# Batch 1 in units of 256 tokens, expert 1 from half-block 8 of batch 1 on, and constant matmuls where TensorE waits in batches 0 and 1

## The chip, the cores and the metric

The kernel runs on one core of one Trainium2 chip. The engines of the core are TensorE (PE, matmuls), VectorE (DVE), ScalarE (ACT), GpSimd (POOL) and SyncE (SP, which here only issues transfers). Each engine works through its own list of instructions in the order of the program and waits on semaphores for the others. The metric is the device time of one execution in microseconds (us).

## What is computed

Eight batches of sliding-window attention with ALiBi, whose output rows are the tokens of a mixture of eight experts; the expert weights come from a Sinkhorn normalisation over all tokens.

```python
batch, n_heads, seq, head_dim = (8, 8, 576, 64)
scores = scale * np.matmul(q, k.transpose(0, 1, 3, 2))
mask = (rel >= 0) & (rel < window)                      # window = 128
scores = np.where(mask, scores + bias[None], -1000000000.0)
attn = np.exp(scores - max); attn = attn / sum
x = matmul(attn, v), as (4608, 512)

P = np.exp(logits)                                      # logits = x @ w_gate, (4608, 8)
for _ in range(8):
    P /= P.sum(1, keepdims=True) + 1e-09
    P /= P.sum(0, keepdims=True) + 1e-09
    P *= N / E
for e in range(E):                                      # w1[e] (512, 1024), w2[e] (1024, 512)
    h = np.maximum(x @ w1[e], 0.0)
    out += P[:, e:e + 1] * (h @ w2[e])
```

Inputs and output are fp32; the matmuls of the kernel take fp16 and accumulate in fp32.

## The kernel before

**Attention.** A batch has 576 tokens, that is four blocks of 128 and one of 64 (kb 0 to 4). Each block is worked in two half-blocks (u) of four heads, so a batch has ten half-blocks; `at = 2 * kb + u` counts them from 0 to 9, and the text writes (b, at). A half-block goes through `scores` (L363, TensorE: keys by queries into the PSUM tile psS), `exps` (L386, ScalarE: exp into pt), `masks` (L398, VectorE: pt times a table that holds both the ALiBi factor and the window), `values` (L409, TensorE: pt by V into psN, where a column of ones gives the sum; VectorE divides into xsb) and, after both halves of a block, `turn_x` (L447), which transposes the block into xT, the input of the experts. For batches 0, 1, 2 and 7 this transpose is done by TensorE (psX, copied by VectorE); for the others by a transposing DMA.

**Getting q, k and v ready.** `load_qk` (L228) loads a batch's q and k in fp32 on the SP queue; `cast_qk` (L237) casts a quarter j of both to fp16, q on VectorE and k on ScalarE; `turn_pe` (L302) transposes one quarter of one of them on TensorE into psT, and ScalarE copies k, VectorE copies q to its place (kN, qN). Batches 0, 1 and 2 go this way; later ones are transposed by DMA. `turn_pe` with j = 4 (NDT) turns the batch's tail of 64 tokens, which ScalarE copies to tT. `load_v` (L330, SP) and `cast_v` (L340, POOL) bring V.

**Experts as filler.** Experts 0 and 1 are worked during attention, in units of some blocks of one expert. A unit (`unit_atoms`, L91) is eight layer-1 steps (`l1`, L97: four matmuls into psh, evicted by ScalarE with a Relu to hT) and one layer-2 step per block (`l2`, L111: eight matmuls into psy, evicted by VectorE in `keep`, L491). `spans` (L502) are the units' blocks, and `order` alternates expert 0 with expert 1 two units behind. `Filler` (L147) hands the steps out: a unit may start when its blocks are ready (`filler.ready`) and its expert is allowed (`filler.allowed`); `fill(us)` issues steps until their planned costs (0.87 us for layer 1 of four blocks, less in proportion for fewer; 1.74 us for layer 2) make up the asked time.

**The order around the change.** The loop over half-blocks (`steps`) issues, in this order: scores of what comes next, its exp, 1 us of filler, its mask, the values of this half-block, the transposes of the block before, the V cast, and then the rest of a budget. The budget is the backlog of filler divided by the half-blocks left up to (b, 8); so at the end of (b, 8) all filler that is ready has been used. Behind the budget stand the events of a half-block: `filler.ready` is raised at every block (L659 to L664), expert 1 is allowed and the first four results are stored at (1, 4), batch 2 is loaded at (0, 3), cast from (1, 3) to (1, 6) and turned from (1, 4) to (1, 7), and the casts of batch b + 2 come at (b, 8), (b, 9) and the two half-blocks after, for b from 1 on.

**Buffers.** The pool `pmm` has four PSUM banks, given out in turn to psT, psN, psX, psh, psy and others; psS has two larger ones. The fp32 loads of V and of the tails share five buffers (`s32`); the large q and k buffers share eight (`a8`).

**After attention** come the Sinkhorn rounds, with the rest of the filler between them, and then experts 2 to 7 in 108 units of 256 tokens (L801 and on).

Of the kernel before, what the change touches and what calls it, by code (L numbers as in the profile page):

```python
# [9 lines left out]
FP16 = mybir.dt.float16  # L10
FP32 = mybir.dt.float32
# [3 lines left out]
def kernel(  # L15
# [10 lines left out]
    nc = tc.nc  # L26
# [9 lines left out]
    P = 128  # L36
# [3 lines left out]
    GT = 512  # L40
    NG = Ntok // GT
# [27 lines left out]
    ident = per.tile([P, P], FP16, name="ident")  # L69
    ident32 = per.tile([P, P], FP32, name="ident32")  # L70
    ones32 = per.tile([P, P], FP32, name="ones32")
    wg_sb = per.tile([P, NDT, E], FP16, name="wg_sb")
    rs_sb = per.tile([P, NBLK], FP32, name="rs_sb")
    cs_sb = per.tile([P, E], FP32, name="cs_sb")
# [72 lines left out]
    class Filler:  # L147


        def __init__(self, units):  # L150
            self.todo = list(units)
            self.l1: list = []
            self.l2: list = []
            self.l1_us = 0.0
            self.since = 0
            self.ready = 0
            self.allowed = {0}

        def start_unit(self):
            for n, (e, b0, nb, make) in enumerate(self.todo):  # L160
# [7 lines left out]
        def take(self):  # L168
            if not self.l1 and len(self.l2) <= 2:
                if self.start_unit():  # L170
                    self.since = 0
            use_l2 = bool(self.l2) and (not self.l1 or self.since >= 2)
            if use_l2:
                self.l2.pop(0)()
                self.since = 0
                cost = L2_US
            elif self.l1:
                self.l1.pop(0)()
                self.since += 1
                cost = self.l1_us  # L180
                if not self.l1:
                    self.l2 = self.l2 + self.next_l2
            else:
                return 0.0
            return cost
# [14 lines left out]
    aps = ctx.enter_context(tc.tile_pool(name="aps", bufs=1, space=bass.MemoryType.PSUM))  # L200
    first_pool = ExitStack()
    asb = first_pool.enter_context(tc.tile_pool(name="asb", bufs=1))
    if True:
# [12 lines left out]
        KT: dict = {}  # L216
        QKT: dict = {}
        vs: dict = {}

        def load_tail(b):  # L220
            t32 = asb.tile([P, H, Dh], FP32, name=f"t32_{b}", tag="s32", bufs=5)
# [187 lines left out]
        def values(b, kb, u):  # L409

            nk, _ = sizes(kb)
            if u == 0:
                xsbs[b, kb] = asb.tile([P, H, Dh], FP16, name=f"xsb_{b}_{kb}", tag="xsb", bufs=3)
            psN = aps.tile([P, GT], FP32, name=f"psN_{b}_{kb}_{u}", tag="pmm", bufs=4)
            psN = psN[:, 0 : 4 * Dh + 4].rearrange("p (h d) -> p h d", h=4)
            ops = []
            for y in range(2):
                for hb in range(2):
                    hh = 2 * y + hb
                    if kb > 0:  # L420
                        ops.append((hh, pts[b, kb - 1, u][:, 2 * hb + y, P : P + nk], vs[b, kb - 1][:, 4 * u + hh, 0 : Dh + 1]))
                    ops.append((hh, pts[b, kb, u][0:nk, 2 * hb + y, 0:nk], vs[b, kb][0:nk, 4 * u + hh, 0 : Dh + 1]))
            if kb == NKB - 1:
                ops = ops[0::2] + ops[1::2]
            for i, (hh, lhsT, rhs) in enumerate(ops):
                nc.tensor.matmul(  # L426
                    out=psN[0:nk, hh, :],
                    lhsT=lhsT,
                    rhs=rhs,
                    start=(i == 0),  # L430
                    stop=(i == len(ops) - 1),
                )
            if kb > 0:
                pts.pop((b, kb - 1, u))
            rden = asb.tile([P, 4], FP32, name=f"rden_{b}_{kb}_{u}", tag="rden", bufs=2)
            nc.vector.reciprocal(out=rden[0:nk, :], in_=psN[0:nk, :, Dh])
            nc.vector.tensor_tensor(
                out=xsbs[b, kb][0:nk, 4 * u : 4 * u + 4, :],
                in0=psN[0:nk, :, 0:Dh],
                in1=rden[0:nk, :].unsqueeze(2).to_broadcast([nk, 4, Dh]),  # L440
                op=ALU.mult,
            )
# [56 lines left out]
            nc.vector.tensor_copy(out=yo, in_=ps)  # L499
            stores.append((e, blk, yo))  # L500

        spans = [(0, 2), (2, 2)] + [(4 * g, 4) for g in range(1, NG)]  # L502
        order = [(0, 0), (0, 1)]
        for n in range(2, len(spans)):
            order += [(0, n), (1, n - 2)]
# [87 lines left out]
        nc.scalar.dma_start(out=rel, in_=rel_h.ap())  # L593
        nc.scalar.dma_start(out=ident, in_=ident_h.ap())
        nc.scalar.dma_start(out=ident32, in_=ident32_h.ap())
        load_first()
        nc.vector.memset(ones32, 1.0)
        make_mask(0)
        cast_v(0)
        load_weights(0, 0, 1)  # L600
# [11 lines left out]
        steps = [(b, kb, u) for b in range(B) for kb in range(NKB) for u in range(2)]  # L612
        for j in range(2):
            cast_qk(0, j)
            turn_pe(0, 1, j)
            turn_pe(0, 0, j)
        cast_qk(0, 2)
        cast_qk(0, 3)
        scores(*steps[0])
        exps(*steps[0])  # L620
        turn_pe(0, 1, 2)
        turn_pe(0, 0, 2)
        masks(*steps[0])
        turn_pe(0, 1, 3)
        turn_pe(0, 0, 3)
        make_mask(1)
        for n, (b, kb, u) in enumerate(steps):
            nxt = steps[n + 1] if n + 1 < len(steps) else None
            at = 2 * kb + u
            left = ((8 if b < XPE else 10) - at) % 10 + 1  # L630
            budget = filler.backlog() / (11 if (b, at) == (XPE, 0) else left)
            if nxt:
                if nxt[0] < XPE and nxt[1:] == (RI - 2, 1):
                    turn_pe(nxt[0], 0, NDT)
                if nxt == (1, 0, 0):
                    cast_qk(1, 0)
                    cast_qk(1, 1)
                    for j in range(NDT):
                        turn_pe(1, 1, j)
                        turn_pe(1, 0, j)  # L640
                        if j < 2:
                            cast_qk(1, j + 2)
                        filler.fill(1.0)
                if n == 0:
                    scores(*nxt)
                elif nxt[2] == 0:
                    scores(*nxt)
                    scores(*nxt[:2], 1)
                exps(*nxt)
            got = filler.fill(1.0)  # L650
            if nxt:
                masks(*nxt)
            values(b, kb, u)
            if n > 0 and u == 0 and by_pe(steps[n - 1][0]):
                turn_x(*steps[n - 1][:2])
            if u == 1 and n // 2 + NKB < B * NKB:
                cast_v(n // 2 + NKB)
            filler.fill(budget - got)
            if at == 0 and b > XPE:  # L659
                filler.ready = 4 * b  # L660
            if at < 8 and b < XPE:
                filler.ready = 4 * b + at // 2
            if at == 8 and b < XPE:
                filler.ready = 4 * b + 4  # L664
            if u == 1 and not by_pe(b):
                turn_x(b, kb)
            if u == 1:
                if kb == 1 and b > 0:
                    gates(4 * b - 4, 4 * b)
                if n // 2 + NKB + 1 < B * NKB:  # L670
                    load_v(n // 2 + NKB + 1)
            if b == 0 and at == 1:
                load_weights(1)
            if b == 1 and at == 4:
                filler.allowed.add(1)
                nc.sync.dma_start(out=ysp[0, 0:RI].rearrange("m p d -> p m d"), in_=first_y[0])
            if (b, at) == (0, 3):
                load_qk(2)
            if (b, at) == (0, 7):
                homes(1)  # L680
            if (b, at) == (1, 3):
                homes(2)
            if b == 1 and 3 <= at <= 6:
                cast_qk(2, at - 3)
            if b == 1 and 4 <= at <= 7:
                turn_pe(2, 1, at - 4)
                turn_pe(2, 0, at - 4)
            if 1 <= b < B - 2 and at == 3:
                load_qk(b + 2)
            if 1 <= b < B - 2 and at >= 8:  # L690
                cast_qk(b + 2, at - 8)
            if 2 <= b < B - 1:
                if at < 2:
                    cast_qk(b + 1, at + 2)
                if at == 1:
                    turn_qk(b + 1)
                    order_qk(b + 1, 1, range(NDT))
                if at == 5:
                    turn_tail(b + 1)
                if at in (6, 7):  # L700
                    order_qk(b + 1, 0, range(2 * at - 12, 2 * at - 10))
            if b < B - 1 and at == (1 if b > 1 else 5) and b:
                load_tail(b + 1)
            if 10 * b + at >= 66:
                i = 10 * b + at - 66
                if i % 8 == 0:
                    home_last(2 + i // 8)
                (load_w2 if i % 8 < 4 else load_w1)(2 + i // 8, i % 4, 4)
            if (b, at) == (7, 0):
                todo += sums_of(2, *extras(2))  # L710
            if b == 7 and at >= 5:
                some(1)
# [30 lines left out]
        for it in range(8):  # L743
# [4 lines left out]
                out=P_sb,  # L748
# [298 lines left out]
```

## Time and profile before

| | |
|---|---|
| median of three runs | 1058.99 us (1057.99 to 1059.68) |
| the profiled execution, its time | 1060.31 us |
| its span, first to last instruction | 1058.5 us |
| PE busy | 1031.1 us (97%), 9006 matmuls |
| DVE, ACT, POOL busy | 631.7, 434.5, 77.4 us |
| DMA | 98.55 MB, mean 93 GB/s |
| ACT evictions of layer 1, 128x512 and 128x256 (36 to 160 us) | mean 599 and 386 ns |

Busy time of PE is the time in which at least one matmul is under way; matmuls are pipelined, so the duration of a group of n matmuls is n times their distance plus the time that the last one takes to drain. The clock in the profile is the share of TensorE's full clock that the throttle granted. A row of the timeline gives start and duration in us, engine, line, operation, output and inputs, shapes and how many instructions were merged; in brackets stands how long the engine was idle before it and what ended that.

### The profile page before, as it was taken

The page shows a single profiled execution, that of the slowest core. Times are in us where ns is not written, and L with a number is a line of the kernel's source. Part 1 is how long each engine was busy: PE and PEld are TensorE (multiplying, and loading weights), DVE is VectorE, ACT ScalarE, POOL GpSimd, SP SyncE. Part 2 cuts the span into 40 slices and gives each one's busy share as a digit, 9 for nine tenths or more (in the row PEclk, how much of TensorE's full clock was granted, in tenths as well). Part 3 has the DMA queues.
Part 4 walks back from the last instruction along what each step waited for, and adds up shares of the span by engine and source line. Part 5 has one row for each costly group of instructions (what it writes and reads, how often), then busy time and mean ns, then how long its engine had stood idle before and what let it go on. Part 6 is the DMA issues. An engine that isn't in the chain of part 4 may idle for free.

```text
span 1058.5 us, 21148 instructions
## 1 busy us (share of the span) xinstructions
PE 1031.1 (97%) x9006; PEld 802.9 (76%) x9006; DVE 631.7 (60%) x1171; ACT 434.5 (41%) x729; POOL 77.4 (7%) x139
## 2 busy tenths in 40 slices
PE   6789999999999999999999999999999999999998
PEld 4455444444544888888888888888888888888887
DVE  4655665655687665655655655655655655555555
ACT  6556555555233333333333333333333333333332
POOL 2112032325100000000000000000000000000000
PEclk9999999999999999999999999999999999999999
DMA  9985599879992501211211210211220220220240
GB/s 226 252 221 139 114 201 218 196 154 177 182 207 70 115 23 49 71 26 46 71 39 33 70 49 23 71 39 32 71 65 7 71 68 3 71 71 1 71 90 20
DMA packets 166110, 98.55 MB, mean 93 GB/s; under 512 B 84960, under 2 KB 157440, under 8 KB 166016
## 3 DMA queue, kind: packets, MB, share of 16 engines
q1 hardware_dynamic: 151280, 79.21, 29.4%
q0 software_dynamic: 14304, 17.84, 10.2%
q8 instruction: 70, 1.15, 0.4%
q14 instruction: 24, 0.20, 0.1%
q10 hardware_dynamic: 432, 0.16, 0.1%
HBM read 87.74 MB, written 19.02 MB: 101 GB/s over the span
## 4 chain that ended last, share of the span: by engine, by line
PE 92%; DMA 4%; SPq 2%; DVE 1%; ACT 1%; issue 0%; POOL 0%; ACTq 0%
PE psh L834 36%; PE psS_m L889 31%; PE psh L102 11%; PE psy L115 10%; DMA v<-in_v_dram 2%; DMA k<-in_k_dram 2%; PE psN L426 1%; PE psS L372 1%; DMA xT<-xsb 1%; SPq L334 1%; SPq L223 0%; SPq L288 0%; PE psy L954 0%; PE psG L473 0%; ACT hT L109 0%
## 5 line engine op out<-in xcount | busy, mean ns | idle before, releaser
L841 ACT ACTIVATE hs<-psh 128x512 f16<-128x512 f32 x432 | 258.0, 597 | 453.2 <-PE psh L834 373.7
L834 PE MATMUL psh<-aux,w1l 128*128 128x256 f16 x2880 | 372.6, 273 | 0.2 <-ACT hs L841 0.2
L834 PEld LDWEIGHTS <-w1l 128*128 128x128 f16 x2880 | 281.7, 98 | 33.3 <-issue 0.5
L889 PEld LDWEIGHTS <-hs 128*128 128x128 f16 x2568 | 251.3, 98 | 29.1
L846 DVE TENSOR_TENSOR hs<-hs 128x1024 f16<-128x1024 f16 x107 | 74.1, 693 | 274.5 <-ACT hs L841 274.3
L889 PE MATMUL psS_m<-w2l,hs 128*128 128x256 f16 x1440 | 186.6, 273 | 0.0
L102 PE MATMUL psh<-xT,w1t 128*128 128x512 f16 (+1 forms) x640 | 141.1, 359 | 4.4 <-DMA xT<-xsb 1.7
L115 PE MATMUL psy<-w2t,hT 128*128 128x512 f16 x576 | 133.8, 379 | 3.4 <-DMA w2t<-in_moe_w_dram 2.8
L818 DVE TENSOR_TENSOR aux<-xT,pbc 128x1024 f16<-128x1024 f16 x108 | 131.4, 1217 | 2.5 <-DMA pbc<-ptd 2.5
L109 ACT ACTIVATE hT<-psh 128x512 f16<-128x512 f32 (+1 forms) x160 | 87.6, 556 | 100.6 <-PE psh L102 99.3
L115 PEld LDWEIGHTS <-hT 128*128 128x128 f16 x576 | 53.7, 98 | 64.6 <-issue 4.8
L102 PEld LDWEIGHTS <-w1t 128*128 128x128 f16 x640 | 57.9, 99 | 53.6 <-issue 6.4
L390 ACT ACTIVATE pt<-psS 128x1024 f16<-128x1024 f32 (+2 forms) x80 | 67.5, 852 | 45.9 <-PE psS L372 37.0
L935 DVE TENSOR_TENSOR acc<-acc,psS_m 128x256 f32<-128x256 f32 (+1 forms) x162 | 74.3, 504 | 12.4 <-PE psS_m L889 11.1
L499 DVE CAST yo<-psy 128x512 f16<-128x512 f32 x68 | 46.9, 690 | 55.5 <-PE psy L115 54.3
L403 DVE TENSOR_TENSOR pt<-pt,mask 128x1024 f16<-128x1024 f16 (+2 forms) x80 | 50.2, 627 | 41.5 <-ACT pt L390 41.4
L889 PE MATMUL psS_m<-more,hs 128*128 128x256 f16 x576 | 74.6, 273 | 0.0
L834 PE MATMUL psh<-aux,w1t 128*128 128x256 f16 x576 | 74.6, 273 | 0.0
L849 DVE TENSOR_TENSOR hs<-hs 128x1024 f16<-128x1024 f16 x107 | 73.2, 684 | 0.0
L834 PEld LDWEIGHTS <-w1t 128*128 128x128 f16 x576 | 56.4, 98 | 6.5
L535 POOL DMA_DIRECT2D w2t<-in_moe_w_dram x2 | 1.8, 878 | 705.2 <-PE psS_m L889 669.8
L426 PEld LDWEIGHTS <-pt 128*128 128x128 f16 (+2 forms) x576 | 28.6, 101 | 26.1 <-DVE pt L403 6.8
(83 smaller groups left out, 657.2 us busy)
## 6 DMA issues: line engine op xcount, KB each, us to landing
pbc<-ptd SPq DMA_DIRECT2D x108, 128.0 KB, 4.5
y<-ysp SPq DMA_DIRECT2D x36, 256.0 KB, 4.7
ysp<-yo SPq DMA_DIRECT2D x68, 128.0 KB, 3.1
v<-in_v_dram SPq DMA_DIRECT2D x32, 256.0 KB, 3.9
out_dram<-acc SPq DMA_DIRECT2D x31, 256.0 KB, 2.4
q<-in_q_dram SPq DMA_DIRECT2D x7, 1024.0 KB, 6.4
k<-in_k_dram SPq DMA_DIRECT2D x7, 1024.0 KB, 9.8
w2t<-in_moe_w_dram POOLq DMA_DIRECT2D x4, 1024.0 KB, 14.7
```

What stands on the lines that cost most here:

```text
L102: nc.tensor.matmul(out=ps[:, 0:nt], lhsT=w1ts[e][:, dt, P * ft : P * ft + P], rhs=xT[:, b0 : b0 + nb, dt, :], start=(dt == 0), stop=(dt == ...
L109: nc.scalar.activation(out=st["hT"][:, ft, 0:nt], in_=ps[:, 0:nt], func=AF.Relu)
L115: nc.tensor.matmul(out=ps, lhsT=st["hT"][:, ft, P * ms : P * ms + P], rhs=w2ts[e][:, ft, :], start=(ft == 0), stop=(ft == NFT - 1),)
L390: nc.scalar.activation(out=pt[0:nk, :, 0 : nk + nn], in_=ps[0:nk, :, :, 0 : nk + nn].rearrange("p a y n -> p (a y) n"), func=AF.Exp, scale ...
L403: nc.vector.tensor_tensor(out=pt[0:nk, :, 0:w], in0=pt[0:nk, :, 0:w], in1=mask[0:nk, hs, 0:w], op=ALU.mult)
L818: nc.vector.tensor_tensor(out=xs(n).rearrange("p (d b t) -> p d b t", d=NDT, b=2), in0=xT[:, 2 * g : 2 * g + 2].rearrange("p b d t -> p d ...
L834: nc.tensor.matmul(out=ps[:, f, :], lhsT=W1L[e][:, dt, P * ft : P * ft + P], rhs=xs(n)[:, HB * dt : HB * dt + HB], start=(dt == 0), stop=( ...
L841: nc.scalar.activation(out=h[n][:, 2 * i : 2 * i + 2, :], in_=ps, func=AF.Relu)
L846: nc.vector.tensor_tensor(out=t[:, NFT : NFT + NF2, :], in0=a[:, 0:NF2, :], in1=a[:, NF2:NFT, :], op=ALU.add)
L849: nc.vector.tensor_tensor(out=t[:, NFT + NF2 : 2 * NFT, :].rearrange("p f n -> p (f n)").rearrange("p (f t) -> p f t", t=P), in0=a[:, :, P ...
L889: nc.tensor.matmul(out=Ms[g, bank][:, half, :], lhsT=left(n, m, f), rhs=W2L[e][RIGHT[m]][:, f, :], start=(e == 2 and f == 0 and half == 0) ...
L935: nc.vector.tensor_tensor(out=a, in0=a, in1=p2, op=op)
```

## The change

- A tile `junk` is made: ones32 read as fp16, 128 x 256. `spin(ps, n)` issues n matmuls of junk by junk, 256 wide, into a given PSUM tile; `spin_alone(n)` does so into a bank of its own from the pool `pmm`. Nobody reads the results. The memset of ones32 moves ahead of the first loads.
- Constant matmuls are issued: 20 at the start, four at each of four places among the first turns, score and masks of batch 0, six ahead of the first layer-2 step, three ahead of each of the four turns of batch 1, and four in `values`, into psN ahead of its own matmuls, in every half-block of batch 0 and in half-blocks 0 to 5 of batch 1. That is 118 in all.
- The four blocks of batch 1 are two units of two blocks instead of one of four, for both experts.
- Expert 1 is allowed at the end of (1, 8) instead of (1, 4).
- The casts of batch 2 move from (1, 3) to (1, 6), one quarter each, to (1, 5) (two quarters), (1, 6) and (1, 7); its turns move from (1, 4) to (1, 7) to (1, 6) (two quarters), (1, 7) and (1, 8), and stand ahead of the casts in each half-block.

```diff
@@ the tiles
     ones32 = per.tile([P, P], FP32, name="ones32")
+    junk = ones32.bitcast(FP16)
@@ class Filler, __init__ and take
             self.allowed = {0}
+            self.begun = False
...
             if use_l2:
+                if not self.begun:
+                    self.begun = True
+                    spin_alone(6)
                 self.l2.pop(0)()
@@ new functions
+        def spin(ps, n):
+
+            for _ in range(n):
+                nc.tensor.matmul(out=ps[:, 0 : 2 * P], lhsT=junk[:, 0:P], rhs=junk, start=True, stop=True)
+
+        spins = [0]
+
+        def spin_alone(n):
+            spins[0] += 1
+            spin(aps.tile([P, GT], FP32, name=f"psJ_{spins[0]}", tag="pmm", bufs=4), n)
@@ values
             psN = aps.tile([P, GT], FP32, name=f"psN_{b}_{kb}_{u}", tag="pmm", bufs=4)
+            if b == 0 or (b == 1 and 2 * kb + u < 6):
+                spin(psN, 4)
@@ the units
-        spans = [(0, 2), (2, 2)] + [(4 * g, 4) for g in range(1, NG)]
+        spans = [(2 * g, 2) for g in range(4)] + [(4 * g, 4) for g in range(2, NG)]
@@ the start
+        nc.vector.memset(ones32, 1.0)
         load_first()
-        nc.vector.memset(ones32, 1.0)
+        spin_alone(20)
         make_mask(0)
...
         for j in range(2):
             cast_qk(0, j)
+            if j:
+                spin_alone(4)
             turn_pe(0, 1, j)
             turn_pe(0, 0, j)
         cast_qk(0, 2)
         cast_qk(0, 3)
+        spin_alone(4)
         scores(*steps[0])
         exps(*steps[0])
+        spin_alone(4)
         turn_pe(0, 1, 2)
         turn_pe(0, 0, 2)
         masks(*steps[0])
+        spin_alone(4)
         turn_pe(0, 1, 3)
@@ ahead of (1, 0)
                     for j in range(NDT):
+                        spin_alone(3)
                         turn_pe(1, 1, j)
                         turn_pe(1, 0, j)
@@ the events of a half-block
+            if (b, at) == (1, 8):
+                filler.allowed.add(1)
             if b == 1 and at == 4:
-                filler.allowed.add(1)
                 nc.sync.dma_start(out=ysp[0, 0:RI].rearrange("m p d -> p m d"), in_=first_y[0])
...
-            if b == 1 and 3 <= at <= 6:
-                cast_qk(2, at - 3)
-            if b == 1 and 4 <= at <= 7:
-                turn_pe(2, 1, at - 4)
-                turn_pe(2, 0, at - 4)
+            if b == 1 and 5 <= at <= 8:
+                for j in ((), (0, 1), (2,), (3,))[at - 5]:
+                    turn_pe(2, 1, j)
+                    turn_pe(2, 0, j)
+                for j in ((0, 1), (2,), (3,), ())[at - 5]:
+                    cast_qk(2, j)
```

## The prediction

> **What bounds the kernel now.** I read the page first: span, busy slices of TensorE (PE) and DMA.
>
> ```profile
> span 1058.5 us, 21148 instructions
> PE   6789999999999999999999999999999999999998
> PEclk9999999999999999999999999999999999999999
> DMA  9985599879992501211211210211220220220240
> ```
>
> A slice is 26.5 us. From the fourth on PE is full, so a change to batches 0 and 1 can only win what PE loses in the first three, where DMA is busy too. Next the busy time in stretches that I cut at the stages (the first pair is length and PE busy; behind POOL come granted clock, DMA share, GB/s):
>
> ```profile
> 0.00:21.50 21.50, 12.80 (x116) 8.31 (x116) 10.37 (x24) 14.85 (x25) 5.90 (x15) 1.00 1.04 225
> ...
> 35.80:42.00 6.20, 5.89 (x66) 4.94 (x66) 4.88 (x9) 5.89 (x14) 3.78 (x8) 1.00 1.06 246
> 42.00:46.60 4.60, 4.60 (x34) 2.20 (x34) 1.79 (x4) 2.35 (x4) 0.00 (x0) 1.00 1.09 273
> 46.60:52.50 5.90, 3.85 (x71) 2.69 (x69) 5.32 (x14) 2.96 (x3) 0.00 (x0) 1.00 1.14 222
> 52.50:55.80 3.30, 0.41 (x8) 0.32 (x9) 0.88 (x4) 1.19 (x3) 0.00 (x0) 0.98 1.21 199
> 55.80:59.30 3.50, 3.50 (x36) 2.80 (x36) 2.59 (x7) 2.92 (x5) 0.00 (x0) 0.53 1.01 177
> ```
>
> PE loses 2.9 us in 52.5:55.8, and right behind it the clock is 0.53. Then the timeline, for who waits there:
>
> ```profile
> 54.62 0.62 ACT L247 CAST c<-k 128x512 f16<-128x512 f32 x1 [2.90 <-DMA k<-in_k_dram]
> 55.77 0.59 PE L457 MATMUL psX<-ident,xsb 128*128 128x128 f16 x4 [2.89 <-ACT tT L320]
> 57.89 1.62 PE L102 MATMUL psh<-xT,w1t 128*128 128x256 f16 x8
> 59.39 0.73 POOL L344 CAST v<-v 128x512 f16<-128x512 f32 x1 [18.12 <-DMA v<-in_v_dram]
> 59.59 2.78 PE L102 MATMUL psh<-xT,w1t 128*128 128x256 f16 x24
> 62.66 1.04 PE L102 MATMUL psh<-xT,w1t 128*128 128x256 f16 x8
> 63.60 0.40 PE L426 MATMUL psN<-v,pt 128*128 128x65 f16 x8
> 73.16 0.61 ACT L247 CAST c<-k 128x512 f16<-128x512 f32 x1
> ```
>
> ScalarE (ACT) stands at the cast of batch 2's k, which lands late; the tail copy (L320) behind it holds PE's next slot. Eight 256-wide matmuls then take 1.62 us instead of 1.04. POOL's cast at 59.39 is V of batch 1, block 3, used by the values at 63.60; the cast at 73.16 is the first of batch 3's k. Last, when that V (issued 38.32) and that k (issued 61.23) landed, from the DMA issues in windows around each:
>
> ```profile
> v<-in_v_dram SPq DMA_DIRECT2D x1, 256.0 KB, 20.9
> ...
> k<-in_k_dram SPq DMA_DIRECT2D x1, 1024.0 KB, 10.0
> ```
>
> That is 59.2 and 71.2 us. Prices: a 256-wide matmul (2.78-1.04)/16 = 0.109 us; 512-wide 0.215 (8 took 1.90, 16 took 3.62); a transpose 0.055 (4 took 0.39, 8 took 0.61). A half unit is so 8 layer-1 steps of 0.435 and two layer-2 steps of 1.72 us. I write (b,n) for half-block n of batch b.
>
> **Part 1, up to 35.8 us: 0.** The 36 constant matmuls at the start, the 6 before the first layer 2, and 4 in each values() of batch 0 cost 0.109 us each, about twice that while cold. The cover is landing: expert 0's w1 lands at 21.5 (issued 12.39, 9.1 us), its w2 at 30.2 (13.87, 16.3 us; PE waited 2.75 us), k of batch 1 at 35.1 (14.43, 20.7 us). Between the last two there are 8 constants, 0.87 us, and PE idles 0.84 us before the turn at 35.84. Bounds 0 to +0.9 if that cover went; I take 0, since the idle row is nearest. Moving the memset ahead of the loads is on VectorE (DVE), 0.17 us beside SP: 0.
>
> **Part 2, 35.8 to 52.5: +1.2 us of delay.** Twelve constants among batch 1's turns are 1.31 us against 0.3 us of PE idle there; ACT, busy 5.89 of 6.20, absorbs none. The four at (0,9) add 0.44 while PE is full. So +0.8 to +1.7; taken 1.2. The later ones (0.44 per half-block) lie under waits for the mask of 0.60, 1.02 and 0.38 us. This delay reaches the end only if PE is not held by a landing next; it is.
>
> **Part 3, casts of batch 2 moved from (1,3) to (1,5): up to -4.** The 2.9 us wait goes, and with it the half clock (0.58 us on the eight matmuls, 0.45 on eight transposes, 1.06 against 0.61: about 1.2 in all). What is late next is V block 3: it lands at 59.2, its cast and memset end at 60.17. PE gets there thus: values(1,4) at 53.7 (52.49 + 1.2); mask, division and copy on DVE make xT by 56.7; six layer-1 steps of expert 0's new half unit 2.6 us, values(1,5) with constants 0.7: 60.0. So values(1,6) start at 60.2, not 63.6. But by 63.6 the old order had done ten layer-1 steps and 16 transposes, the new one six and none: 16 x 0.109 + 16 x 0.055 = 2.6 us are still to do. Net -3.4 + 2.6 = -0.8 us. No queue is passed: SP still issues in the same order, so both landings stay; the casts stand now behind the exp of (1,6), and pass nothing on POOL.
>
> **Part 4, expert 1 from (1,8): +2.0.** (1,5) to (1,8) hold 7 us of filler instead of 14, so they end sooner. From 60.2: values, turn, two layer-1 steps and four turns 2.3; (1,7) 2.7 and (1,8) 2.7 with one layer-2 step each: 67.9, with short waits about 68.1 instead of 76.7. At its end ACT is given batch 3's k cast, which was at 73.16 after a landing at 71.2: now ACT stands from 68.6 to 71.3. Behind it are exp(2,0) (1.02 us) and the evictions of layer 1. PE runs scores (0.9 with their wait), two layer-1 steps, values, one more step, until 70.9; the fourth needs the first one's PSUM buffer, evicted after cast 0.61, exp 1.02 and 0.39: 73.4. That is 2.5 us. If the half-blocks run 1.5 us slower than summed, it is 1.0; if layer-2 steps (evicted by DVE) were in line, near 0. I take 2.0, nearer to the upper end because the next filler is eight layer-1 steps in a row. That a k wait can be covered shows here:
>
> ```profile
> 145.91 1.90 PE L115 MATMUL psy<-w2t,hT 128*128 128x512 f16 x8
> 147.33 0.62 ACT L247 CAST c<-k 128x512 f16<-128x512 f32 x1 [5.18 <-DMA k<-in_k_dram]
> ```
>
> There PE had layer 2 to run; at (1,9) it has none.
>
> **Part 5, 256-wide units: +0.2.** For two experts 128 matmuls of 0.109 replace 64 of 0.215: +0.19. ACT's evictions, 32 of 386 ns for 16 of 599, add 2.8 us beside PE, where ACT was busy 9.75 of 13.3 in 76.7:90; if all of it got onto the path, +2.8; the 35 us of filler spread over ten half-blocks hide it.
>
> At (2,8) both orders have used up all filler, so from (2,9) on they are the same program. Short waits of PE after 63.6 (0.6, 0.5 and 0.4 us) come again.
>
> **Sum:** 0 - 0.8 + 2.0 + 0.2 = +1.4 us. The profiled execution took 1060.31 us (span 1058.5 and 1.8 around it), 1.3 above the median of 1058.99; the same step on the median gives 1060.4.
>
> **Rivals.** *Faster (1056.1).* The k of batch 3 does not hold PE and V block 3 is in time: then -2.9 - 1.2 + 1.2 = -2.9 with all else 0. For it: landings vary, and unprofiled runs are 1.3 us shorter. Against it: DMA is busy without a break to 78 us, so nothing lands earlier by the change.
>
> *Faster by a warm start (1053.6).* Eight transposes took 1.03 us at 5.3 against 0.61 later, so PE is slow until 21.5. If that stage were PE's, its 12.80 us busy would shrink by 0.42 of it, 5.4 us. Against: w1 lands at 21.5 and PE's first load of it waited for just that. The Trainium skill, "TensorE: Matmul & The Clock Gate", "What's actually happening", says the clock is half until some 3.4 us of activity; by that the 20 constants warm PE before the first scores. The trace agrees on the half speed, but not that the time would follow.
>
> *Slower (1062.1).* PE's clock falls at the new wait, as it did after 2.9 us idle at 52.9: 3.5 us at 0.53 cost 1.7, so +3.1. No constants stand at (1,9). It decides from a gap between 2.75 us (27.6 to 30.3, clock stayed 1.00) and 2.89 (fell). The same page, "Why this matters for your kernels", allows gaps up to about 3 us; by it this rival never comes, but the row fell at 2.89, and the measurement decides.
>
> **How the numbers follow.** I call within 0.2% (2.1 us) the same, about what a measurement can tell. Forecast 0.52 (own range 1058.4 to 1061.1); first rival 0.18; warm start 0.03; slower 0.27, which takes in more of ACT's 2.8 us or the start's 0.9 on the path. That is faster 0.21, same 0.52, slower 0.27. The range goes down to the first rival's price and up past the slower one's by half of part 1's bound: 1056.2 to 1062.7.
>
> **What would show it.** Right: no wait of the tail copy near 52, clock 1.00 from 50 to 60, values(1,6) within 1 us of POOL's cast near 60, an ACT cast waiting 2 to 3 us for k near 71, PE waiting 1 to 2.5 us for hT right behind it, (2,9) within 3 us of before. Wrong: PE full from 60 to 75, or values(1,6) long after the cast, or waits after (2,9) that were not there.

## The result, and the profile after

The changed kernel took 1064.23 us (median of five runs, 1063.2 to 1067.59), the kernel before 1058.99 us beside it. The ratio is 1.0054, with a 95% interval from 1.0035 to 1.0072: slower by half a per cent, above the range of the prediction. The profiled execution took 1063.87 us. All medians and ratios leave out two executions of pair_warm below (1232.33 and 2755.55 us), which ran far slower than all others.

Span, busy slices and DMA of the changed kernel's page:

```profile
span 1062.1 us, 21527 instructions
PE   8989999999999999999999999999999999999998
PEclk8999999999999999999999999999999999999999
DMA  9996299779993502201201211211210220220240
```

PE is busier in the first two slices (8 and 9 tenths, where it was 6 and 7) and no busier in the third; part of that is the constants themselves, and the span is 3.6 us longer all the same. The stretches of before, cut at the same times, of the kernel after (length, busy PE, PEld, DVE, ACT and POOL, granted clock, DMA share, GB/s):

```profile
0.00:21.50 21.50, 18.32 (x172) 12.72 (x172) 10.66 (x24) 14.90 (x25) 5.56 (x15) 0.92 1.02 224
...
35.80:42.00 6.20, 5.70 (x69) 4.91 (x67) 5.18 (x12) 5.22 (x11) 3.76 (x8) 1.00 0.93 242
42.00:46.60 4.60, 4.60 (x43) 3.04 (x41) 1.09 (x3) 4.07 (x8) 0.00 (x0) 1.00 1.06 264
46.60:52.50 5.90, 5.40 (x62) 3.53 (x59) 4.84 (x12) 1.94 (x2) 0.00 (x0) 1.00 1.13 229
52.50:55.80 3.30, 3.25 (x59) 2.68 (x57) 2.88 (x9) 1.62 (x3) 0.00 (x0) 1.00 1.21 197
55.80:59.30 3.50, 1.83 (x31) 1.48 (x28) 2.01 (x5) 1.85 (x3) 0.00 (x0) 1.00 1.24 217
```

The hole of before at 52.5:55.8 is closed (3.25 us busy where it was 0.41), and the clock is 1.00 from 50 to 60. But in 55.8:59.3, where PE was busy throughout before, it now idles 1.67 us. Now the timeline of the changed kernel for the places that the prediction named, and for batch 2:

```profile
55.44 0.41 PE L444 MATMUL psN<-v,pt 128*128 128x65 f16 x8
58.38 1.03 PE L103 MATMUL psh<-xT,w1t 128*128 128x256 f16 x8 [1.26 <-DVE xT L483]
59.93 1.91 PE L103 MATMUL psh<-xT,w1t 128*128 128x256 f16 x16
60.30 0.61 POOL L360 CAST v<-v 128x512 f16<-128x512 f32 x1 [18.54 <-DMA v<-in_v_dram]
61.68 0.41 PE L444 MATMUL psN<-v,pt 128*128 128x65 f16 x8
63.45 1.03 PE L103 MATMUL psh<-xT,w1t 128*128 128x256 f16 x8 [1.14 <-ACT hT L110]
72.24 0.62 ACT L263 CAST c<-k 128x512 f16<-128x512 f32 x1 [0.27 <-DMA k<-in_k_dram]
74.43 3.67 PE L103 MATMUL psh<-xT,w1t 128*128 128x256 f16 x32
77.54 0.61 ACT L263 CAST c<-k 128x512 f16<-128x512 f32 x1
78.05 1.03 ACT L406 ACTIVATE pt<-psS 128x1024 f16<-128x1024 f32 x1
78.38 0.10 PEld L116 LDWEIGHTS <-hT 128*128 128x128 f16 x1
78.97 0.66 ACT L110 ACTIVATE hT<-psh 128x256 f16<-128x256 f32 x2
79.40 1.89 PE L116 MATMUL psy<-w2t,hT 128*128 128x512 f16 x8 [0.96 <-ACT hT L110]
84.51 2.78 PE L103 MATMUL psh<-xT,w1t 128*128 128x256 f16 x24
88.59 1.89 PE L116 MATMUL psy<-w2t,hT 128*128 128x512 f16 x8 [0.84 <-ACT hT L110]
98.69 1.89 PE L116 MATMUL psy<-w2t,hT 128*128 128x512 f16 x8 [0.54 <-ACT hT L110]
```

V's cast stands where the prediction put it (60.30), but `values` of (1,6) start at 61.68, 1.4 us after it started. The wait for k is 0.27 us, not 2.7. What was not forecast stands below these rows: in batch 2, PE stands three times in front of a layer-2 step. The releaser reads "hT", but the weights of that step, which are hT, had been loaded at 78.38; what the matmul at 79.40 still lacked was its PSUM bank. By the order in which `pmm` hands out its four banks, it had held the first layer-1 step of the next unit, whose eviction (78.97) stood on ACT behind a cast and an exp. That this is the cause is what the paired kernels below test. In the waits of PE from (1,9) to (2,9), first before, then after (engine, line, releaser: total us, times, longest):

```profile
PE psh L102 <- DVE xT L465: 0.5, 1, 0.5
PE psh L102 <- ACT hT L109: 0.4, 1, 0.4
```

```profile
PE psy L116 <- ACT hT L110: 2.3, 3, 1.0
```

**Where the 3.6 us arise.** I compare the time at which DVE starts the division behind each `values`. (1,0) is 2.5 us later than before (48.00 to 50.52). (1,9) is 4.3 us earlier (78.85 to 74.54), but with less filler done: 23 fewer 256-wide matmuls (2.5 us) and 21 fewer 512-wide ones (4.5 us), 7.0 us in all. So at (1,9) the kernel is behind by 2.7 us, nearly what it was at (1,0): the middle of batch 1 won nothing and lost next to nothing. At (2,9), where both have used up their filler, it is 4.8 us behind (115.50 to 120.30): batch 2 cost another 2.1 us. From there the shift stays at 4.8 until (3,4), falls to 3.5 by (4,0), and ends at 3.6. Around (4,0) the kernel before waited 1.7 us for a transposing DMA, which the later one did not; why that DMA was in time was not traced.

### The profile page after: what moved, and what is told of

Its sections match the earlier page's. It is cut to its first block, busy times and chain, and to the rows that moved or that the text cites. A ratio compares the mean times of both kernels' runs of the same rounds, so it can differ in the third digit from the quotient of the medians.

```text
span 1062.1 us, 21527 instructions
## 1 busy us (share of the span) xinstructions
PE 1043.9 (98%) x9188; PEld 819.5 (77%) x9188; DVE 633.2 (60%) x1171; ACT 437.3 (41%) x745; POOL 78.6 (7%) x139
## 4 chain that ended last, share of the span: by engine, by line
PE 84%; DMA 1%; DVE 0%; issue 0%; SPq 0%; DVEq 0%
PE psh L861 35%; PE psS_m L916 31%; PE psy L116 8%; PE psh L103 8%; PE psN L444 1%; DMA pbc<-ptd 1%; PE psS L388 1%; PE psy L981 0%; PE psG L491 0%; DVE yo L517 0%; DVE aux L845 0%; PE psX L475 0%; PE psC L786 0%; DVE pt L419 0%; PE psP L801 0%
## 5 line engine op out<-in xcount | busy, mean ns | idle before, releaser
L110 ACT ACTIVATE hT<-psh 128x512 f16<-128x512 f32 (+1 forms) x176 | 89.9, 521 | 110.1 <-PE psh L103 108.1
L116 PEld LDWEIGHTS <-hT 128*128 128x128 f16 x576 | 53.7, 98 | 64.2 <-issue 4.5
L103 PEld LDWEIGHTS <-w1t 128*128 128x128 f16 x704 | 64.7, 99 | 49.9 <-issue 5.7
L861 PEld LDWEIGHTS <-w1t 128*128 128x128 f16 x576 | 56.4, 98 | 6.5
L916 PEld LDWEIGHTS <-aux 128*128 128x128 f16 x428 | 41.9, 98 | 4.8
## 6 DMA issues: line engine op xcount, KB each, us to landing
k<-in_k_dram SPq DMA_DIRECT2D x7, 1024.0 KB, 10.2
```

The source lines that it names most:

```text
L103: nc.tensor.matmul(out=ps[:, 0:nt], lhsT=w1ts[e][:, dt, P * ft : P * ft + P], rhs=xT[:, b0 : b0 + nb, dt, :], start=(dt == 0), stop=(dt == ...
L110: nc.scalar.activation(out=st["hT"][:, ft, 0:nt], in_=ps[:, 0:nt], func=AF.Relu)
L116: nc.tensor.matmul(out=ps, lhsT=st["hT"][:, ft, P * ms : P * ms + P], rhs=w2ts[e][:, ft, :], start=(ft == 0), stop=(ft == NFT - 1),)
L861: nc.tensor.matmul(out=ps[:, f, :], lhsT=W1L[e][:, dt, P * ft : P * ft + P], rhs=xs(n)[:, HB * dt : HB * dt + HB], start=(dt == 0), stop=( ...
L916: nc.tensor.matmul(out=Ms[g, bank][:, half, :], lhsT=left(n, m, f), rhs=W2L[e][RIGHT[m]][:, f, :], start=(e == 2 and f == 0 and half == 0) ...
```

## The experiments

Two theories stood at the start. Theory 1: the constants in batches 0 and 1 lie on PE's path and make the 2.5 us up to (1,0). Theory 2, called U later: the half units of batch 1 cost the time, as their small layer-1 steps fill ACT and the PSUM banks. Theory E, added after the first runs: it is the late start of expert 1 that costs. In the ratios, the kernel before that ran beside each one is 1, and the brackets hold the 95% interval. Every kernel here, also where it is called the kernel before with one edit, has the memset of ones32 ahead of the loads.

**no_const: the change without any constant.**

```diff
         def spin(ps, n):
-            for _ in range(n):
+            for _ in range(0):
...
         def spin_alone(n):
-            spins[0] += 1
+            return
```

> The changed kernel without any of its 118 constant matmuls; units, expert 1's start and casts as changed. Theory 1 (constants on the path): of 12.9 us of constants some 8.2 lay in waits and 4.6 pushed work back (half-block (1,0) came 2.5 us later); without them (1,0) is back at 48 us and the kernel takes 1064.2 - 4.6 = 1059.6 us, or up to 1.5 more if V of block 3 (near 60 us) and k of batch 3 (near 71 us) now hold TensorE as predicted. Theory 2 (the new order and the 256-token units cost the time, the constants are free): 1063 to 1065 us.

Measured 1063.37 us, 1.0035 [1.0017, 1.0052]. By the medians the constants are about a third of the loss (1.0054 to 1.0035), and the two intervals overlap. Theory 1 expected 1059.6 to 1061.1 us. The three waits of batch 2 are here as they were, to the hundredth (timeline, PE):

```profile
78.08 1.89 PE L116 MATMUL psy<-w2t,hT 128*128 128x512 f16 x8 [0.96 <-ACT hT L110]
...
87.26 1.89 PE L116 MATMUL psy<-w2t,hT 128*128 128x512 f16 x8 [0.84 <-ACT hT L110]
...
97.38 1.89 PE L116 MATMUL psy<-w2t,hT 128*128 128x512 f16 x8 [0.54 <-ACT hT L110]
```

**const_only: the kernel before with the constants alone.** All calls of `spin` and `spin_alone`, and none of the other edits.

```diff
+        spin_alone(20)
         make_mask(0)
...
+            if b == 0 or (b == 1 and 2 * kb + u < 6):
+                spin(psN, 4)
```

> The kernel before with the 118 constant matmuls alone. Theory 1: (1,0) 2.5 us later, but the 2.9 us wait for batch 2's k at 52 to 54.6 us takes most of that up, so 1059 to 1061 us, less than the constants cost in the changed kernel, where this wait is gone. Theory 2: 1059 us, no change. A clock that falls less often would show as under 1058.

Measured 1060.33 us, 1.0008 [0.9995, 1.0021]. This fits the range of theory 1 too, which had the wait for k take up the delay: the profile shows (1,0) 3.5 us later than before and (1,6) only 0.7. What speaks against theory 1 as the main cause is no_const. By const_only, 118 constants, 12.9 us of PE at 0.109 us each, are worth about 0.1% at the end, and the interval includes none.

**casts_only: the moved casts and turns of batch 2 alone.** The kernel before with the last hunk of the diff.

```diff
-            if b == 1 and 3 <= at <= 6:
-                cast_qk(2, at - 3)
...
+                for j in ((0, 1), (2,), (3,), ())[at - 5]:
+                    cast_qk(2, j)
```

> The kernel before with batch 2's casts and turns alone moved to half-blocks 5 to 8. Both theories: the wait of the tail copy near 52 us and the half clock behind it go, 2.9 + 1.2 us, and expert 1's filler keeps TensorE full until V lands; 1055.5 to 1057.5 us. If a later landing takes the gain, 1058 to 1060.

Measured 1059.49 us, 1.0000 [0.9987, 1.0013]. The wait for k goes here as well, and the time does not move. By the divisions in the profiles, the stretch from (1,0) to (1,9) is 1.6 us shorter than before with the same filler, but (1,0) came 1.4 us later, in a part that this edit does not touch. So the moved casts win something where they stand, less than the 4.1 us expected. The clock fell here too, only earlier (51.5 to 54.9 us):

```profile
52.50:55.80 3.30, 3.00 (x48) 2.50 (x46) 1.67 (x6) 1.99 (x3) 0.00 (x0) 0.64 1.23 200
```

PE is busy for 3.00 of the 3.30 us that were a hole, but at 0.64 of its clock.

**units_only: batch 1 in half units alone**, with expert 1 still from (1,4), no constant, casts as before.

```diff
-        spans = [(0, 2), (2, 2)] + [(4 * g, 4) for g in range(1, NG)]
+        spans = [(2 * g, 2) for g in range(4)] + [(4 * g, 4) for g in range(2, NG)]
```

> The kernel before with batch 1 in units of two blocks alone (expert 1 still from (1,4)). Theory 1: 64 matmuls of 512 become 128 of 256, +0.2 us, and the waits of layer 2 for the last eviction of a unit come twice as often, four more of 0.5 to 1 us: 1059 to 1062. Theory 2: most of the 5.2 us, 1062 to 1065.

Measured 1067.07 us, 1.0066 [1.0048, 1.0084]. This one line alone costs as much as the whole change, more than either theory had for it. Half units are ready sooner, so filler goes out in batch 1 that the kernel before kept for batch 2 (96 matmuls of layer 2 by the division of (1,9), where before had 64), and at the end of batch 2 there is too little. Stretches around it, of this kernel:

```profile
109.30:116.40 7.10, 5.46 (x59) 2.98 (x57) 6.11 (x16) 2.28 (x6) 5.44 (x8) 1.00 0.94 284
116.40:122.10 5.70, 4.62 (x30) 1.98 (x31) 3.63 (x12) 2.03 (x3) 0.67 (x2) 0.70 1.16 220
122.10:128.00 5.90, 5.65 (x25) 2.30 (x24) 1.50 (x6) 3.28 (x6) 1.38 (x4) 0.71 0.24 63
```

PE idles 1.64 and 1.08 us in the first two, and the clock is at half from 118.7 to 125.5.

**old_units: the change with the units of before.** The `spans` line undone; constants, casts and the late expert 1 stay.

```diff
-        spans = [(2 * g, 2) for g in range(4)] + [(4 * g, 4) for g in range(2, NG)]
+        spans = [(0, 2), (2, 2)] + [(4 * g, 4) for g in range(1, NG)]
```

> The changed kernel with batch 1 again as one unit of four blocks: constants, moved casts and expert 1 from (1,8) stay. Theory U (the 256-token units cost the time, by twice as many PSUM banks and evictions): the waits of layer 2 for a bank behind cast and exp in batch 2 (0.96, 0.84 and 0.54 us) go, but (1,5) to (1,8) have no filler and run at the pace of ScalarE and VectorE, near 1.5 us a half-block; 1060 to 1062 us. Theory E (expert 1's late start costs the time): 1064 or more, since this order has even less to do there.

Measured 1066.16 us, 1.0061 [1.0048, 1.0075]: no better than the change, so the units cannot be blamed by undoing them. Here V block 3 does hold PE at (1,6), as the prediction had it for the change itself. Timeline and stretches of old_units:

```profile
60.79 0.55 PE L444 MATMUL psN<-v,pt 128*128 128x65 f16 x7 [3.30 <-POOL v L361]
```

```profile
54.50:61.40 6.90, 3.19 (x58) 2.78 (x56) 4.44 (x15) 3.95 (x6) 1.06 (x3) 0.87 1.12 183
61.40:66.90 5.50, 5.25 (x62) 4.44 (x60) 4.56 (x12) 3.35 (x7) 2.25 (x8) 0.55 0.93 283
```

PE waits 3.30 us, and the clock is 0.55 for the next five. The parts of the change do not add up one by one: with expert 1 late, the unit of four blocks leaves PE without filler here, and with expert 1 early, the half units leave it without at the end of batch 2.

**early_expert: the change with expert 1 from (1,4).**

```diff
-            if (b, at) == (1, 8):
+            if (b, at) == (1, 4):
                 filler.allowed.add(1)
```

> The changed kernel with expert 1 from (1,4) again. Theory U with its second part (smaller units are ready earlier, so 21 us of filler go into (1,5) to (1,8) and the end of batch 2 has none, idle and at half clock as with the units alone): 1065 to 1068 us. Theory E: 1059 to 1061.

Measured 1065.72 us, 1.0064 [1.0046, 1.0083]. Theory E falls: with half units, the early expert is no better. By counts of matmuls, 22.7 us of filler go out between the divisions of (1,4) and (1,8), where before had 12.4, and the clock is at half from 119.1 to 122.5 in batch 2, as in units_only.

**pair_bank: the change, with two layer-1 steps of a half unit in one PSUM bank.** The matmuls are the same; 16 evictions of 128x512 replace 32 of 128x256, and the planner sees one step of 0.87 us. Batch 0's half units, which the kernel before has too, stay single.

```diff
+        def l1_two(i):
+            ps = pool.tile([P, 2, nt], FP32, name=f"psh_{e}_{b0}_{i}", tag=tag[0], bufs=bufs[0])
+            for f in range(2):
+                ft = 2 * i + f
...
+            nc.scalar.activation(out=st["hT"][:, 2 * i : 2 * i + 2, 0:nt], in_=ps, func=AF.Relu)
...
+        if nb == 2 and b0 >= 4:
+            first = [lambda i=i: l1_two(i) for i in range(NFT // 2)]
```

> The changed kernel, but batch 1's two-block units put two layer-1 steps into one PSUM bank and evict them with one 128x512 instruction, planned as one step of 0.87 us. Same matmuls, half the banks and evictions. Theory U by banks: the three waits of layer 2 in batch 2 and the 1.1 us wait at (1,6) go, 1064.2 - 2 to 3 = 1061 to 1062. If the matmuls of 256 or the order itself cost the time: 1064 as changed.

Measured 1061.32 us, 1.0014 [1.0002, 1.0026], down from 1.0054: the two intervals are apart. (2,9) is 1.1 us behind before instead of 4.8; 0.7 of these 3.7 us stand already at (1,0), ahead of the first paired step, and are not its work. From (1,9) to (2,9), this kernel and the changed one:

```profile
73.60:116.50 42.90, 42.71 (x397) 28.43 (x397) 23.97 (x54) 23.18 (x42) 9.63 (x18) 1.00 0.62 149
```

```profile
74.50:120.30 45.80, 43.27 (x398) 28.77 (x398) 23.36 (x55) 24.37 (x54) 10.21 (x18) 1.00 0.55 141
```

The same work takes 2.9 us less: PE's idle time is 0.2 us instead of 2.5, and ACT has 42 instructions instead of 54. PE's waits there in pair_bank:

```profile
PE psy L116 <- ACT hT L139: 0.2, 1, 0.2
```

**pair_step: two layer-1 steps handed out together**, as one planned step of 0.87 us, but still in two banks with two evictions. This parts the order of the steps from banks and evictions.

```diff
+        def l1_both(i):
+            l1(2 * i)
+            l1(2 * i + 1)
...
+        if nb == 2 and b0 >= 4:
+            first = [lambda i=i: l1_both(i) for i in range(NFT // 2)]
```

> The changed kernel with two layer-1 steps of batch 1's units handed out together, as one planned step of 0.87 us, but each still in its own PSUM bank with its own eviction of 256. The order of the work is that of the run with paired banks. If the banks and evictions cost the time: 1064, as changed (1063 to 1065.5). If the order of the steps did: 1061 to 1062, as with paired banks.

Measured 1062.82 us, 1.0031 [1.0021, 1.0042]. So of the 0.40% between the change and pair_bank, about 0.23 is the order and 0.17 the banks and evictions; the intervals of neighbours just touch or overlap, so that both have a part is likely, and their sizes are rough. In the profiles the stretch from (1,9) to (2,9), with the same filler, takes 45.8 us in the changed kernel, 44.7 here and 42.9 in pair_bank: there the banks and evictions have the larger part. Two waits stay in this kernel from (1,9) to (2,9), now of a layer-1 step for its bank:

```profile
PE psh L103 <- ACT hT L110: 1.5, 2, 1.0
```

The order matters because `Filler` lets a layer-2 step through when two layer-1 steps have gone since the last. In a half unit these two are 0.87 us of PE, not 1.74; a unit's two layer-2 steps are used up early, and a row of six layer-1 steps follows (the 24 matmuls at 84.51 above). In pair_step four layer-1 steps stand between two of layer 2, at the same place:

```profile
82.57 1.05 PE L103 MATMUL psh<-xT,w1t 128*128 128x256 f16 x8
83.45 0.29 PE L451 MATMUL psN<-v,pt 128*128 128x65 f16 x4
83.58 1.03 PE L103 MATMUL psh<-xT,w1t 128*128 128x256 f16 x8
84.45 1.89 PE L116 MATMUL psy<-w2t,hT 128*128 128x512 f16 x8
```

The first wait of batch 2 is not a matter of this order: in pair_step too it follows a row of 32 layer-1 matmuls and lasts 0.96 us. Of the two later ones, that of 0.84 us, which stood behind the row of 24, is gone, and that of 0.54 stays.

**pair_all: paired banks for all half units, batch 0's too, and no constant.** The condition is `if nb == 2:`, and `spin` is empty as in no_const.

> As the run before, for batch 0's units too, and without the constants. Theory U by banks, with the constants worth the 0.9 us that two comparisons gave: 1060 to 1061 us, and below 1059 if the moved casts win what the trace showed at 52 to 59 us. Otherwise as without constants: 1063.

Measured 1059.15 us, 1.0002 [0.9993, 1.0011]. This is the change without its constants and without its bank trouble, and it is level with the kernel before. Against no_const (1.0035) pairing, that is banks, evictions and order together, is worth 0.33%, and the intervals are apart.

**pair_warm: pair_all with the 24 constants of `values` in (1,0) to (1,5).**

```diff
-            if b == 0 or (b == 1 and 2 * kb + u < 6):
+            if b == 1 and 2 * kb + u < 6:
                 spin(psN, 4)
```

> Paired banks for all units of two blocks, casts and expert 1 as changed, and of the constants only the 24 in half-blocks 0 to 5 of batch 1, which lie under waits for the mask. Paired without constants took 1059.2 and had a clock of 0.5 from 50.7 to 60.9 us, some 2 us of loss. If these constants hold the clock: 1056.5 to 1058.5. If a landing (V near 60 us, k near 71) takes it: 1058.5 to 1060.

Measured 1061.08 us (median of ten executions), 1.0019 [1.0004, 1.0034]. The times fall in two groups, five of 1059.6 to 1059.9 and five of 1062.2 to 1063.8 us; what parts them is not in the profile, which is of the lower group (span 1058.0 us, as in pair_all). This run settles nothing.

**casts_pair and casts_pair_warm: what is left when the costly parts are out.** The kernel before with the moved casts and paired banks for batch 0's two half units; batch 1 stays one unit of four blocks, expert 1 from (1,4). The second has the 24 constants of pair_warm too.

```diff
+        if nb == 2:
+            first = [lambda i=i: l1_two(i) for i in range(NFT // 2)]
...
+                for j in ((0, 1), (2,), (3,), ())[at - 5]:
+                    cast_qk(2, j)
```

> The version that beat the kernel before (moved casts, paired banks for batch 0's units, 24 constants in batch 1), now without the constants. If holding the clock at 50 to 60 us is what let the moved casts win: back to no difference, 1058.5 to 1060. If the paired banks of batch 0 did it: 1057.5 as with them.

> The kernel before with the moved casts, paired banks for batch 0's two units, and the same 24 constants; batch 1 as one unit of four blocks and expert 1 from (1,4). The moved casts alone made no difference, with the clock falling at 51.5 us in the profiled run. If the clock was what took their gain: 1056.5 to 1058. If a landing: 1058.5 to 1060.

Measured 1058.22 us, 0.9983 [0.9971, 0.9994], and 1057.69 us, 0.9980 [0.9968, 0.9992]. Both beat the kernel before, by about 0.2%, and the constants make no difference between them, though in their profiles the clock stayed full from 50 to 60 us with them and fell from 49.5 to 52.9 without. Stretches of casts_pair:

```profile
46.60:52.50 5.90, 4.28 (x64) 2.93 (x64) 5.19 (x14) 2.96 (x3) 0.00 (x0) 0.75 1.16 222
52.50:55.80 3.30, 2.61 (x39) 2.09 (x38) 1.75 (x8) 2.22 (x3) 0.00 (x0) 0.93 1.21 197
```

PE is busy 2.61 us where before it was 0.41, though at clocks of 0.75 and 0.93. Paired banks on the kernel before alone were not run, and 0.9983 stands against 1.0000 for the casts alone with intervals that overlap, so how the gain divides stays open.

## Why the prediction was wrong

The sum had the right sign, +1.4 us, and about a quarter of the size: the medians differ by 5.2 us, the two profiled executions by 3.6. The sign was luck: it came from the +2.0 of part 4, which measured 0, and without that term the sum would have been -0.6. By the profiles, 1.6 us of these arise in part 1, 1.0 in part 2, 0.2 in parts 3 and 4 together and 2.1 in batch 2, and 1.3 come back later.

- **Part 5 failed, and with it the number.** The step was: ACT's evictions add 2.8 us beside PE, and "the 35 us of filler spread over ten half-blocks hide it", +0.2. Batch 2 cost 2.1 us in the profiles, and pairing the banks took the whole kernel from 1.0054 to 1.0014. I had counted ACT's time as a sum over a stage, but PE waits for one bank at one moment: a step half as long holds its bank nearly as long as a full one when its eviction queues behind a 1.03 us exp. I also passed over the count of steps in `Filler`, which turns half-size steps into another order. "Short waits come again" failed with it: before had 0.9 us of them from (1,9) to (2,9), after had 2.3 in another place.
- **Part 1 was taken at 0 and came out, on average, at its upper bound.** At (0,8) the profiles of the six kernels with all constants are 0.9 to 2.5 us behind before, 1.4 on average; the six without (before is one) are at -0.3 to +1.6, on average 0.5. The difference is 0.9, the bound that I had set and not taken. It is small against the spread, which the drops of the clock and the landings make (w1 at 21.3 to 23.1 us in these kernels).
- **Part 2 had the delay right and its end wrong.** From (0,8) to (1,0), each of the six kernels with constants lost 0.96 or 0.97 us; forecast was 1.2, between 0.8 and 1.7 (its own terms, 1.31 less 0.3 and plus 0.44, make 1.45). But the step "This delay reaches the end only if PE is not held by a landing next; it is." failed: V's cast ended at 60.91, and PE had filler to run until 61.68. The price at the end is about 0.1% for all constants together: 0.08 alone, 0.19 between the change and no_const, 0.12 between pair_bank and pair_all (where batch 0's units are paired too), each with an interval wider than itself.
- **Part 3 was right in what goes, wrong in what that is worth.** The wait for k and the half clock behind it went. V landed at 60.15 (59.2 before) and its cast ended at 60.91, but `values` of (1,6) started at 61.68, not 60.2: PE was still in 16 layer-1 matmuls. The walk to that place had its lengths right, 6.2 us from the values of (1,4) to those of (1,6) where 6.3 were summed; it started at 55.44 and not at 53.7, as parts 1 and 2 had cost 2.5 us by (1,0) and not 1.2. And the end of one wait was not the end of waiting: between the divisions of (1,0) and (1,9) PE idled 5.1 us before and 4.2 after, as waits of 1.26 us for xT, 1.14 for an eviction and 0.75 for q's copy took the place of the 2.9. The 0.9 us and the 1.2 of the half clock about paid for the 19 constants in that stretch, 2.1 us. The wait for V that I expected came in old_units, where `values` of (1,6) start at 60.79 after 3.30 us.
- **Part 4 had the right wait at the wrong size.** ACT did wait for batch 3's k, 0.27 us where 2.7 was summed, and PE lost nothing to it. k landed at 72.2 (71.3 before), but ACT came to that place at 72.0, 3.4 us later than my sum said. The term of +2.0 measured 0.
- **The rivals.** *Faster* had its conditions met, as no landing held PE, and the time went up; its sum lacked part 5. *Warm start* was right that the clock could be full early, at 7.0 us; but w1 landed at 23.0 (21.5 before), and PE stood idle for 1.73 us until then, so the landing ended that stage, as the prediction had argued. *Slower* had the sign and another mechanism: the clock stayed at 1.00 from (1,9) to (2,9). What it describes came elsewhere, in old_units behind the wait of 3.30 us and in units_only behind 116.4.

## What to carry to other kernels

Halving a step halves its matmul time, but not the number of PSUM banks, evictions and places in the planner that it takes; price a smaller step by what it holds at one moment (a bank until the slowest engine in front of its eviction is through), not by the sums of engine time in the stage. If smaller units are needed for readiness, put two steps into one bank, evict them at once and hand them out as one step. Constant matmuls that keep an engine busy while it waits for a landing bought nothing at the landing here, and filler that is ready sooner is missing later, where the next hole may cost a clock drop.

## What was not expected of the hardware

**Constants make the clock full early, and it falls again anyway.** In the kernel before, the record shows the first rise to full at 21.55 us; in the changed kernel at 7.0, with matmuls on the constant from 1.1 us on. In the six kernels with all constants it stands at 4.9 to 7.0 us, in the other eight at 19.6 to 25.6. But the clock fell again from 13.85 to 17.26, and from 24.1 to 27.5 us, right behind the wait for w1 (landed at 23.0). The first two stretches of the changed kernel, with granted clocks of 0.92 and 0.81:

```profile
0.00:21.50 21.50, 18.32 (x172) 12.72 (x172) 10.66 (x24) 14.90 (x25) 5.56 (x15) 0.92 1.02 224
21.50:30.30 8.80, 7.24 (x70) 5.84 (x71) 3.58 (x11) 3.70 (x11) 0.65 (x2) 0.81 1.20 244
```

The row of before for 0 to 21.5 says 1.00, although eight transposes in it took 1.03 us instead of 0.61, so the record seems to begin with the first change.

**The drops come in one length.** In the profiles, a fall (but for the one behind the last matmuls) lasts 3.41 us or a small multiple of that (6.8 in units_only at 118.7, 10.2 in pair_all at 50.7), and starts at places that differ from kernel to kernel. The Trainium skill, "TensorE: Matmul & The Clock Gate", "What's actually happening", gives a free-running window of 3413 ns; the trace agrees with that length.

**A drop does not need an idle time of 3 us.** In const_only the clock fell at 30.7, after PE had waited 2.06 us for w2 (timeline and stretch of const_only):

```profile
30.56 3.45 PE L116 MATMUL psy<-w2t,hT 128*128 128x512 f16 x8 [2.06 <-DMA w2t<-in_moe_w_dram]
```

```profile
30.30:35.80 5.50, 5.24 (x26) 2.42 (x27) 1.42 (x4) 0.74 (x2) 0.00 (x0) 0.69 1.15 237
```

Eight matmuls that take 1.89 us at full clock took 3.45. The same page of the Trainium skill, "Why this matters for your kernels", allows gaps up to about 3 us; here the clock fell right behind 2.06 us, and in the kernel before it did not behind 2.75 us at 27.6, so no gap length by itself tells whether the clock will fall. Nor does the work in a stretch of 3.41 us laid on the clock's changes: all 24 falls of the 14 profiles follow one in which PE was busy 0.4 to 2.1 us (1.35 here, from 27.3 to 30.7), but the kernel before was busy 1.47 from 28.4 to 31.8 and its clock stayed full. A stretch busier than 2.1 us was in no profile followed by a fall.
